# Pooled attention and four causal experts on one core: the same steps under two written-out orders

## The chip, the core and the metric

The kernel runs on one core of a Trainium2 chip. The core has a matmul engine (TensorE, PE in the profile; its weight loads are shown as PEld), VectorE (DVE), ScalarE (ACT), GpSimd (POOL) and SyncE (SP), each with an instruction stream of its own that runs in order and waits on semaphores; sixteen DMA engines move data. The metric is the device time of the program in microseconds. The kernel before took 159.37 us, the median of three runs (159.12 to 161.31).

## The reference

Inputs are q, k, v of 8 batches, 8 heads, 576 rows, 64 columns in fp32. First an attention whose keys and values are averaged over groups of eight rows, then a mixture of four small causal attention experts on its output x, of which each row uses the best two:

```python
def _attn_ref(q, k, v):
    k_p = k.reshape(B, H, Sp, pool, D).mean(axis=3)      # pool = 8, 72 keys
    v_p = v.reshape(B, H, Sp, pool, D).mean(axis=3)
    attn = softmax(scale * np.matmul(q, k_p.transpose(0, 1, 3, 2)))
    return np.matmul(attn, v_p)                          # becomes x: B, 576, 512
def _moe_ref(x, w_gate, wq, wk, wv, wo):
    logits = x @ w_gate                                  # 4 experts, the best 2 weigh in
    for e in range(E):
        q, k, v = x @ wq[e], x @ wk[e], x @ wv[e]        # 64 columns each
        a = softmax(causal(scale * (q @ k.transpose(0, 2, 1))))
        out += weight_of_e * (a @ v @ wo[e])
    return out                                           # B, 576, 512 in fp32
```

## The kernel before, in words

Each batch goes through a chain of some 140 small steps. A step is a Python function that issues a few instructions on one engine, and has a short name; `E1:2@46` is step E, part 1, of batch 2, with its PSUM banks 4 to 7. A letter d behind a copy puts it on DVE and not on ACT, a letter c behind a matmul step cuts it into tiles 32 columns wide.

- L_k, L_q, L_v (`load`, L118) are the loads of a batch, issued on POOL; they turn fp32 into bf16 on the way and write three rotating buffers a kind. W0 to W4 load the weights.
- PK, PV average k and v by a matmul; kc, kt, vc bring the result to SBUF. u (`turn`, L255) transposes q on DVE.
- E0, E1, E2 (`Es`) are the scores of rows 0 to 511 of one half of the heads, of the other, and of the last 64 rows of all (in batch 0: of rows 0 to 255, 256 to 511 and the rest); e00 to e21 (`es`, L292) their exponentials on ACT; D, d, x the sums and their inverses; O, o (`ov`, L338) the output x, transposed.
- P, p are the experts' q and k by pairs of experts; V, v their values and the gate's logits; g0 to g9 the gate; S, s (`sb`, L462) the experts' scores and exponentials; a (`am`, L479) the causal mask on POOL; B (`Bv`) the weighted values, bz, bg, b (L514 to L521) their scaling into the tile osc.
- osc must be transposed for the output projection. For batches 0, 1, 6 and 7 that is T (`flip`, L198, on PE) and a copy t; for batches 2 to 5 it is F (`crossbar`, L546 and L549), a transposing DMA issued on SP. F00 and F10 carry the main rows of the two expert pairs, F01 and F11 the last 64 rows.
- Y (`Y`) is the output projection of 128 rows (rows 512 to 575 of two batches share Y4), y (`y`, L180) the copy of its result into ofin, and with it the store on SP (`z`, L584, L580), 256 KB each. The last stores partly go out on ACT's queue.
- H is a warm-up: a matmul on a constant tile, whose result nothing reads (`warm_up`, L177).

All matmuls but the warm-ups and T stand on one helper line, L189. They come in tile shapes: 128*128 (rows by columns of the array) for P, V, B, T, Y and H, 64*128 for S, 32*128 for E, 96*32 for PK, PV, D and O.

The order in which steps are issued is one list of tokens, SEQ, written out in full, and a loop that calls each token's function. PE, ACT, DVE and POOL run their instructions in exactly that order (`manual_schedule`); SP's list follows the order of the F and y tokens. The list comes from a planner outside the kernel, which gives each step a cost and each buffer a time at which it is free; the kernel holds only its result. Batches overlap: while the experts of batch b run, the first attention of b+1 and b+2 is under way.

Of the kernel before, what the change touches and what calls it, by code (L numbers as in the profile page):

```python
# [21 lines left out]
def kernel(  # L22
# [553 lines left out]
    def z(b, c, queue):  # L576
# [17 lines left out]
        H1:0@0 u10:0 L_k2:1 u11:0 u01:0 E2:0@02 u00:0 E1:0@46 L_q0:1 e21:0 e20:0 e11:0 E0:0@02 L_q1:1 e10:0 PV:0@6  # L594
        L_q2:1 e01:0 vc:0d e00:0 c1:0d O11:0@6 L_q3:1 D1:0@7 c0:0d d1:0 O00:0@0 O20:0@1 O10:0@2 x1:0 D0:0@7 c2:0d W2:0
        O01:0@3 c3:0d D2:0@4 d0:0 H1:0@5 o11:0 d2:0 o10:0 W3:0 x2:0 x0:0 o20:0 P_q01:0@2 o00:0 L_v0:1 P_k01:0@1 p_q01:0
        o01:0 P_t0:0@0 p_k01:0 P_q11:0@2 L_v1:1 p_t0:0 P_q10:0@1 p_q11:0 L_v2:1 P_k11:0@0 p_q10:0 PK:1@2 p_k11:0 W4:0
        S02:0@4 kc:1 S03:0@0 S12:0@6 s02:0 P_k10:0@3 L_k0:2 kt:1d P_q00:0@2 u0:1 s03:0 L_k1:2 s12:0 H1:0@4 H1:0@4 u1:1
        a02:0 p_q00:0 p_k10:0d E2:1@04 L_k2:2 c4:0d E0:1@26 e20:1 e21:1 L_q0:2 V3:0@0 e01:1 V0:0@1 L_q1:2 v3:0d e00:1
        E1:1@46 a12:0 v0:0d V2:0@0 L_q2:2 e10:1 V1:0@1 v2:0d L_q3:2 PV:1@2 e11:1 v1:0d D0:1@0 a03:0 D2:1@3 vc:1d  # L600
        P_k00:0@4 L_v0:2 d0:1 D1:1@1 g1:0 O01:1@2 p_k00:0d x0:1 O00:1@0 L_v1:2 g2:0 S00:0@4 d1:1 o01:1 S10:0@6 x1:1
        O20:1@1 L_v2:2 g3:0 o00:1 O10:1@2 d2:1 s10:0 o10:1 O11:1@3 PK:2@0 L_k0:3 o11:1 x2:1 s00:0 S11:0@6 o20:1 L_k1:3
        S01:0@2 kc:2 P_t0:1@1 s11:0 g4:0 L_k2:3 kt:2d V2:1@0 p_t0:1d s01:0 V4:1@4 L_q0:3 v2:1d V3:1@1 u1:2 P_q0:1@0
        v4:1 L_q1:3 v3:1 g0:0 u0:2 a11:0 E1:2@24 p_q0:1 L_q2:3 g5:0 B11:0@1 g6:0 e10:2 g7:0 a10:0 P_k0:1@0 bz11:0
        L_q3:3 g8:0 g9:0 e11:2 bg11:0 E0:2@26 b11:0 a00:0 p_k0:1d L_v0:3 B10:0@1 e00:2 P_k1:1@4 bz10:0 a01:0 bg10:0
# [36 lines left out]
        e21:7 D0:7@0 b10:4 O00:7@2 e20:7 O20:6@6 d0:7 D1:7@7 O11:7@4 F10:4 o20:6 D2:7@1 O10:7@5 x0:7 g1:6 O20:7@0
        P_k0:6@6 d2:7 o00:7 x2:7 d1:7 P_t0:6@1 o20:7 x1:7 o01:7 P_k1:6@2 p_t0:6 o10:7 p_k0:6 B00:4@3 p_k1:6 S10:5@0
        bz00:4 S12:5@6 bg00:4 Y4:1@5 o11:7 s10:5 V4:7@2 b00:4 F11:4 s12:5 V0:7@4 y4:1d a10:5 F01:4 Y2:1@3 F00:4 v4:7d
        v0:7 S01:5@0 a12:5 y2:1d g0:6 S11:6@6 S11:5@4 s01:5 V3:7@2 g2:6 g3:6 V2:7@3 s11:6 v3:7d a01:5 Y3:3@0 v2:7d
        Y4:3@2 s11:5 y3:3d a11:6 V1:7@3 y4:3d B01:5@1 v1:7 S03:5@4 a11:5 S00:6@6 bz01:5 S01:6@2 s03:5 bg01:5 P_k0:7@0
        b01:5 s00:6 a03:5 g1:7 g2:7 B10:5@1 g4:6 p_k0:7 g5:6 a00:6 g6:6 Y3:2@6 s01:6 bz10:5 P_k1:7@7 bg10:5 b10:5 y3:2
# [83 lines left out]
```

## Time and profile before

| | |
|---|---|
| median of three runs | 159.37 us |
| the profiled execution | 159.26 us, span 157.6 us from the first to the last instruction |
| granted clock of the core, mean | 0.969 |
| PE, ACT, DVE, POOL busy | 91%, 85%, 79%, 57% of the span |
| read from HBM, written | 30.42 MB, 9.44 MB |

The profile is one execution. A busy PE there is not PE at its peak, since matmuls are pipelined and their ends are modelled; so starts of matmuls are compared, not lengths. A row of the chain of waits gives start, length and what the time went to; a row of the ordered list gives start, length, engine, line, operation, output and inputs, shape, and in brackets how long the engine stood idle before it and what ended that. The time of a run holds some 1.7 us around the span (159.26 - 157.6).

### The profile page before, as it was taken

The numbers are of one execution on the slowest core, as the hardware profiler recorded it, in microseconds if no ns is written. First come the engines' busy times: TensorE is split into PE (matmuls) and PEld (weight loads), VectorE is DVE, ScalarE is ACT, GpSimd is POOL, SyncE is SP. The second block draws the span as 40 slices with busy tenths as digits, with TensorE's granted clock in tenths as the row PEclk, the third lists the DMA queues.
The fourth block names the chain that finished last, engine by engine and source line by source line (L and its number), as shares of the span: only waits on it lengthen the run. The fifth ranks groups of instructions, "written<-read, shape, count | busy, mean of one in ns | idle before, by whom it ended". The sixth has DMA issues, their size and how long they took to land.

```text
span 157.6 us, 5500 instructions
## 1 busy us (share of the span) xinstructions
PE 143.9 (91%) x2155; PEld 82.8 (53%) x2155; DVE 124.4 (79%) x412; ACT 133.7 (85%) x249; POOL 90.5 (57%) x162
## 2 busy tenths in 40 slices
PE   6876798988999999999999899999999999999940
PEld 2333565545456356446545564857576665557620
DVE  1513567697999989998999889999998998898840
ACT  3016778999899999999999899999999999899740
POOL 6997479976989799897986342004500343533000
PEclk9998579999999999999999999999999999999996
DMA  2999999999999999999999994512213064487994
GB/s 19 161 173 180 181 179 179 188 179 182 180 182 180 180 180 181 178 249 181 180 245 249 179 148 108 37 50 60 80 28 104 8 177 131 124 320 264 344 354 146
DMA packets 70635, 26.20 MB, mean 166 GB/s; under 512 B 65744, under 2 KB 66000, under 8 KB 70608
## 3 DMA queue, kind: packets, MB, share of 16 engines
q0 software_dynamic: 60240, 15.21, 99.7%
q1 hardware_dynamic: 10144, 10.23, 21.2%
q10 hardware_dynamic: 224, 0.39, 0.9%
q8 instruction: 17, 0.28, 0.7%
q14 instruction: 10, 0.08, 0.2%
HBM read 30.42 MB, written 9.44 MB: 253 GB/s over the span
## 4 chain that ended last, share of the span: by engine, by line
PE 53%; DMA 23%; POOL 14%; issue 3%; DVE 2%; POOLq 0%; DVEq 0%
PE psum L189 52%; DMA kraw<-in_k_dram 18%; DMA qraw<-in_q_dram 5%; POOL kraw L118 4%; POOL vraw L118 3%; POOL qraw L118 3%; POOL etb L479 2%; PE psum L198 1%; POOL wst_q L131 1%; POOL wst_k L131 1%; DVE qT L255 1%; POOL wop L131 0%; DVE osc L521 0%; DVE ofin L180 0%; DVE G L406 0%
## 5 line engine op out<-in xcount | busy, mean ns | idle before, releaser
L462 ACT ACTIVATE etb<-psum 128x1024 bf16<-128x1024 f32 x48 | 47.6, 1033 | 1.1 <-PE psum L189 1.0
L479 POOL TENSOR_SCALAR_AFFINE_SELECT etb<-etb 128x256 bf16<-128x256 bf16 x64 | 25.5, 412 | 37.9 <-ACT etb L462 36.7
L292 ACT ACTIVATE eta<-psum 96x1024 bf16<-96x1024 f32 (+1 forms) x48 | 36.1, 812 | 4.7 <-PE psum L189 4.2
L118 POOL DMA_DIRECT2D qraw<-in_q_dram x32 | 21.2, 669 | 4.8 <-DMA vraw<-in_v_dram 2.2
L189 PEld LDWEIGHTS <-etb 128*128 128x128 bf16 x480 | 18.7, 97 | 7.2 <-issue 2.8
L338 DVE TENSOR_TENSOR xT<-psum,rza 128x512 bf16<-128x512 f32 x32 | 20.8, 684 | 1.7 <-ACT rza L315 1.4
L118 POOL DMA_DIRECT2D vraw<-in_v_dram x24 | 18.6, 777 | 6.2 <-DMA kraw<-in_k_dram 3.6
L189 PE MATMUL psum<-vaug,etb 128*128 128x65 bf16 x480 | 20.6, 193 | 0.1
L189 PE MATMUL psum<-xT,wqp 128*128 128x64 bf16 (+2 forms) x136 | 20.2, 282 | 0.1
L189 PE MATMUL psum<-wvg,xT 128*128 128x260 bf16 x144 | 20.0, 274 | 0.1
L189 PE MATMUL psum<-wop,oT 128*128 128x512 bf16 (+1 forms) x74 | 19.8, 374 | 0.2 <-DVE oT L180 0.2
L189 PE MATMUL psum<-xT,wkp 128*128 128x64 bf16 (+2 forms) x136 | 19.8, 279 | 0.0
L118 POOL DMA_DIRECT2D kraw<-in_k_dram x24 | 18.6, 785 | 1.7 <-POOLq L715 0.8
L521 DVE TENSOR_TENSOR osc<-psum,gt 128x256 bf16<-128x256 f32 (+2 forms) x40 | 16.5, 421 | 1.0
L189 PEld LDWEIGHTS <-xT 128*128 128x128 bf16 x144 | 12.7, 97 | 7.2 <-issue 3.7
L189 PE MATMUL psum<-qk 64*128 64x64 bf16 (+4 forms) x192 | 15.6, 277 | 0.2 <-ACT etb L462 0.2
L189 PE MATMUL psum<-eta,vp 96*32 96x64 bf16 (+2 forms) x272 | 14.1, 301 | 1.1 <-DVE vp L180 0.8
L189 PE MATMUL psum<-qT,kpT 32*128 32x64 bf16 (+2 forms) x272 | 12.7, 281 | 2.6 <-DVE qT L255 2.3
L255 DVE STREAM_TRANSPOSE qT<-qraw 128x576 f32<-128x576 f32 (+2 forms) x18 | 11.9, 690 | 3.7 <-DMA qraw<-in_q_dram 3.5
L180 ACT COPY ofin<-psum 128x512 f32<-128x512 f32 (+1 forms) x22 | 12.6, 591 | 1.6 <-PE psum L189 1.5
L180 DVE CAST qk<-psum 128x512 bf16<-128x512 f32 (+1 forms) x22 | 13.3, 611 | 0.7 <-PE psum L189 0.6
L315 ACT ACTIVATE rza<-rza 128x512 f32<-128x512 f32 (+1 forms) x24 | 12.5, 529 | 0.3
(75 smaller groups left out, 216.5 us busy)
## 6 DMA issues: line engine op xcount, KB each, us to landing
out_dram<-ofin SPq DMA_DIRECT2D x31, 256.0 KB, 3.5
kraw<-in_k_dram POOLq DMA_DIRECT2D x24, 192.0 KB, 7.8
qraw<-in_q_dram POOLq DMA_DIRECT2D x32, 144.0 KB, 7.6
vraw<-in_v_dram POOLq DMA_DIRECT2D x24, 192.0 KB, 7.2
out_dram<-ofin SPq DMA_DIRECT2D x7, 128.0 KB, 2.6
wst_q<-in_moe_wq_dram POOLq DMA_DIRECT2D x1, 256.0 KB, 7.4
wst_k<-in_moe_wk_dram POOLq DMA_DIRECT2D x1, 256.0 KB, 8.0
wst_v<-in_moe_wv_dram POOLq DMA_DIRECT2D x1, 256.0 KB, 8.3
```

Of the source, the lines that this page charges most:

```text
L118: nc.gpsimd.dma_start(out=dst, in_=src)
L131: nc.gpsimd.dma_start(out=dst, in_=src)
L180: (nc.vector.tensor_copy if dve else nc.scalar.copy)(out=out, in_=in_)
L189: nc.tensor.matmul(out=out, lhsT=lhsT, rhs=rhs, start=start, stop=stop)
L198: nc.tensor.transpose(out=out[s], in_=in_[:, s], identity=ident[0:n, 0:n])
L255: nc.vector.transpose(out=dst.rearrange("p (a s n) -> p a n s", s=32, n=2), in_=src.rearrange("p (a n d) -> p a n d", n=2, d=32))
L292: nc.scalar.activation(out=dst, in_=src, func=EXP, scale=ATT_EXP_SCALE)
L315: nc.scalar.activation(out=rz, in_=rz, func=EXP, scale=-1.0)
L338: nc.vector.tensor_tensor(out=xT[:, 2 * got[0][0] + t : 2 * got[-1][0] + t + 1 : 2, m + got[0][1].start : m + got[0][1].stop], in0=psum[:, ...
L462: nc.scalar.activation(out=et[:, ep, :, eo : eo + n], in_=psum[:, bank : bank + 2, 0:n], func=EXP, scale=MOE_EXP_SCALE,)
L479: nc.gpsimd.affine_select(out=blk, in_=blk, pattern=[[0, 2], [1, 128]], compare_op=ISGE, fill=0.0, base=0, channel_multiplier=-1,)
L521: nc.vector.tensor_tensor(out=osc(b, ep)[:, own, :].rearrange("p c (e d) -> p e c d", e=2), in0=o[:, :, :, 0:HD], in1=gt.to_broadcast([128 ...
```

## The change

Only SEQ changes: 1098 tokens become 1106. Every step of the old list is in the new one once, and eight warm-ups more (24 in place of 16), of which seven are in the form with 32 columns that the old list does not use. The first tokens, to the first loads of batch 1, are the same; behind them the order is different on every engine:

- In the planner, stores and crossbar transfers have a higher cost, a change of tile shape on PE has one, and output projections of older batches come earlier; the new list is what it then wrote. On PE the list changes shape 113 times before and 111 times after.
- Of the copies from PSUM, 29 move from DVE to ACT and 26 from ACT to DVE.
- Some PSUM banks are other ones.
- The order of the loads among themselves is the same; where they stand between POOL's masks is not.
- On SP, the six stores ahead of the first transfer were y1:0, y3:0, y0:0, y1:1, y3:1, y2:0 and are y3:0, y1:0, y2:0, y1:1, y0:0, y3:1; the transfers of batches 2 and 3 stand together, with only y0:2 between them.

The lines of both lists that hold the steps named below:

```diff
--- before
+++ after
@@ the list SEQ in the kernel @@
...
-        H1:0@0 u10:0 L_k2:1 u11:0 u01:0 E2:0@02 u00:0 E1:0@46 L_q0:1 e21:0 e20:0 e11:0 E0:0@02 L_q1:1 e10:0 PV:0@6
...
-        O01:0@3 c3:0d D2:0@4 d0:0 H1:0@5 o11:0 d2:0 o10:0 W3:0 x2:0 x0:0 o20:0 P_q01:0@2 o00:0 L_v0:1 P_k01:0@1 p_q01:0
...
-        E1:1@46 a12:0 v0:0d V2:0@0 L_q2:2 e10:1 V1:0@1 v2:0d L_q3:2 PV:1@2 e11:1 v1:0d D0:1@0 a03:0 D2:1@3 vc:1d
-        P_k00:0@4 L_v0:2 d0:1 D1:1@1 g1:0 O01:1@2 p_k00:0d x0:1 O00:1@0 L_v1:2 g2:0 S00:0@4 d1:1 o01:1 S10:0@6 x1:1
...
-        S01:0@2 kc:2 P_t0:1@1 s11:0 g4:0 L_k2:3 kt:2d V2:1@0 p_t0:1d s01:0 V4:1@4 L_q0:3 v2:1d V3:1@1 u1:2 P_q0:1@0
-        v4:1 L_q1:3 v3:1 g0:0 u0:2 a11:0 E1:2@24 p_q0:1 L_q2:3 g5:0 B11:0@1 g6:0 e10:2 g7:0 a10:0 P_k0:1@0 bz11:0
...
-        bg02:1 O10:3@0 b11:1 y3:0 PV:4@1 b02:1 s00:2 o10:3 a02:2 E0:4@26 vc:4d PK:5@0 L_k0:6 e01:4 g1:2 T11:1@4
...
-        L_q0:7 o00:4 y3:1 PV:5@6 y2:0 kc:6 L_q1:7 O01:4@7 S02:3@4 vc:5 o01:4 E0:5@02 a10:2 s02:3 L_q2:7 g7:2 V4:3@6
...
-        D0:5@5 bg11:2 O10:5@2 b11:2 e20:5 PK:7@3 vc:6d x1:5 F11:2 S10:3@0 d0:5 S12:3@6 F10:2 o10:5 V3:4@4 s10:3 kc:7
...
-        F11:3 y2:2 S01:4@0 a11:4 F10:3 p_t0:5d S00:4@4 S10:4@6 s01:4 g5:4 V4:5@2 g6:4 g7:4 g8:4 V3:6@3 s10:4 v4:5d
...
-        b11:4 V0:6@2 bz01:4 Y0:2@3 e10:7 bg01:4 b01:4 V2:6@0 y0:2d B10:4@1 v2:6 E2:7@46 v0:6 O01:7@3 bz10:4 bg10:4
...
-        g7:6 S10:6@4 F11:5 g8:6 a01:6 p_k1:7d g0:7 S02:6@0 S12:6@2 s10:6 B00:5@6 g9:6 g3:7 g4:7 g5:7 P_q0:7@7 s12:6
...
-        Y0:4@7 y0:3d s00:7 Y2:3@1 a10:7 B11:6@0 y0:4d S02:7@4 y2:3 a00:7 bz11:6 S11:7@2 bg11:6 S12:7@6 s02:7 b11:6
-        Y3:5@1 g8:7 g9:7 Y1:5@0 s11:7 y3:5d a02:7 Y4:5@4 B00:7@5 y1:5d B01:6@1 y4:5 a11:7 T11:6@2 s12:7 Y0:5@3 bz01:6
...
-        bz12:7 Y2:7@3 bg12:7 y3:7 b12:7 T02:6@6 T02:7@5 T12:6@2 T12:7@7 y2:7p t02:6d t02:7d t12:6d t12:7d Y4:7@0 z2:7
...
+        H1:0@0 H1:0@0 u00:0 H1:0@0 L_k2:1 u01:0 u10:0 E0:0@02 u11:0 L_q0:1 E1:0@46 e00:0 H1:0@0c L_q1:1 H1:0@0c H1:0@0c
...
+        O00:0@5 W2:0 O10:0@2 c2:0d e20:0 D0:0@3 o10:0 O20:0@0 d0:0 O11:0@1 D2:0@6 W3:0 o11:0 d2:0 x2:0 x0:0 P_q01:0@1
...
+        S03:0@0 S12:0@2 kc:1 s03:0 W4:0 P_k00:0@4 s12:0 kt:1d P_q10:0@5 L_k0:2 p_k00:0d P_q00:0@0 p_q10:0 P_k10:0@1
+        u1:1 L_k1:2 p_q00:0 P_k01:0@5 p_k10:0 u0:1 a12:0 E1:1@26 p_k01:0 E2:1@04 L_k2:2 e10:1 c4:0d H1:0@2c H1:0@2c
...
+        P_t0:1@1 g5:0 kt:2d L_q0:3 V3:1@2 v4:1d s02:0 P_q0:1@3 u1:2 L_q1:3 v3:1 u0:2 a11:0 E1:2@46 p_t0:1 p_q0:1 L_q2:3
...
+        O00:2@7 d2:2 kc:3 O10:2@2 x1:2 S02:1@0 o00:2 L_k2:4 S01:1@4 kt:3 B01:0@3 s02:1 o11:2 V2:1@7 L_q0:4 bz01:0 o10:2
...
+        p_q1:4 t02:0d u0:6 E2:5@06 D0:5@4 v1:4 PK:7@2 e21:5 g2:3 e20:5 D1:5@3 g3:3 d0:5 O10:5@5 kc:7 O00:5@0 d1:5
...
+        g4:4 V3:6@1 g1:5 g5:4 u1:7 Y0:2@0 s00:4 a01:4 B11:3@4 v3:6d V0:6@5 y0:2d s11:4 V2:6@1 a00:4 bz11:3 P_t0:5@6
+        bg11:3 g0:5 b11:3 v2:6 B01:3@0 a11:4 v0:6 p_t0:5d F10:3 S02:4@2 x2:6 bz01:3 S10:4@4 bg01:3 S03:4@6 s02:4
...
+        E1:7@26 bz11:4 bg11:4 Y4:1@0 b11:4 e10:7 a00:5 g2:6 Y0:1@4 y4:1d F11:4 Y2:3@1 e11:7 B10:4@5 y0:1d Y2:2@0 bz10:4
...
+        b10:5 y0:3 a00:6 B11:5@4 y2:4d g0:7 S03:7@0 S02:7@2 S12:6@6 s03:7 bz11:5 F11:5 Y3:2@5 bg11:5 b11:5 s12:6 a03:7
...
+        S10:7@0 bg10:6 s00:7 Y4:5@4 b10:6 g8:7 Y0:4@5 g9:7 s10:7 y4:5d Y3:3@6 a00:7 B11:6@7 y0:4d s01:7 Y3:4@4 a10:7
...
+        Y0:6@1 t02:6d t01:7 bz12:7 B02:7@4 bg12:7 y0:6 b12:7 Y3:7@5 bz02:7 t12:6 Y2:7@6 bg02:7 b02:7 y3:7 T02:7@4
+        T12:7@7 y2:7p t02:7d t12:7d Y4:7@0 z2:7 ya4:7 yb4:7d
```

More of the change, by code (lines that the diff above doesn't have):

```diff
@@ L643 @@
[L643 to L647, printed above, removed]
@@ new lines @@
+        p_q0:4d E0:5@02 g0:3 y0:0 u1:6 a11:3 T12:1@6 B10:2@4 L_v1:7 e00:5 P_k1:4@5 t12:1d bz10:2 bg10:2 e01:5 L_v2:7
+        b10:2 E1:5@06 p_k1:4d V3:4@4 a02:3 e10:5 kt:6d Y3:1@5 a01:3 v3:4d P_q1:4@2 e11:5 y3:1d T02:0@4 g1:3 V1:4@3
+        p_q1:4 t02:0d u0:6 E2:5@06 D0:5@4 v1:4 PK:7@2 e21:5 g2:3 e20:5 D1:5@3 g3:3 d0:5 O10:5@5 kc:7 O00:5@0 d1:5
+        S12:4@6 g4:3 B11:2@2 g5:3 x0:5 g6:3 g7:3 V2:4@3 x1:5 g8:3 bz11:2 g9:3 T02:1@4 o00:5 P_k0:4@1 s12:4 o10:5
+        B01:2@0 t02:1 v2:4 a12:4 bg11:2 p_k0:4 b11:2 S03:3@4 S00:3@6 bz01:2 D2:5@3 s03:3 F11:2 bg01:2 O01:5@2 b01:2
@@ new lines @@
+        PV:6@1 d2:5 s00:3 a03:3 o01:5 O20:5@3 O11:5@0 V0:4@4 F10:2 o11:5 vc:6 B10:3@2 a00:3 v0:4 kt:7d E1:6@06 x2:5
+        g0:4 F01:2 o20:5 V3:5@4 e11:6 bz10:3 bg10:3 P_k0:5@3 v3:5d e10:6 b10:3 E0:6@46 p_k0:5d F11:3 B00:2@2 e00:6 u0:7
+        V0:5@0 P_k1:5@3 bz00:2 e01:6 bg00:2 b00:2 B00:3@1 v0:5d p_k1:5 F00:2 E2:6@46 D0:6@0 bz00:3 bg00:3 e20:6 O10:6@3
+        b00:3 PV:7@2 e21:6 d0:6 g1:4 O01:6@4 F01:3 O00:6@1 vc:7d D1:6@5 x0:6 D2:6@0 O11:6@6 g2:4 V1:5@7 d1:6 o00:6
+        P_q0:5@2 x1:6 o01:6 d2:6 v1:5 V2:5@1 o10:6 p_q0:5 V4:5@0 o11:6 v2:5 S01:4@4 v4:5 S11:4@2 g3:4 S00:4@6 s01:4
@@ new lines @@
+        y2:3 B00:4@4 bg10:4 b10:4 y2:2 E2:7@26 D0:7@1 bz00:4 e20:7 D1:7@5 bg00:4 b00:4 O11:7@0 e21:7 F10:4 O20:6@2 d1:7
+        O01:7@3 O10:7@6 o20:6 O00:7@4 x1:7 g3:6 D2:7@5 O20:7@7 P_k0:6@2 g4:6 d0:7 o10:7 d2:7 P_k1:6@1 x2:7 o11:7 x0:7
+        o20:7 p_k0:6 B01:4@6 o01:7 p_k1:6 V4:7@7 o00:7 g0:6 S02:5@2 v4:7 S01:5@0 bz01:4 S10:5@4 bg01:4 s02:5 b01:4
+        V0:7@7 g5:6 F01:4 V3:7@6 g6:6 s01:5 v0:7d a02:5 P_q0:7@2 v3:7d s10:5 g7:6 F00:4 a01:5 V1:7@3 p_q0:7d P_t0:6@6
+        v1:7 g8:6 a10:5 S11:5@0 p_t0:6d S03:5@4 S12:5@2 s11:5 g9:6 P_k0:7@7 s03:5 V2:7@6 a11:5 s12:5 p_k0:7d Y1:3@0
@@ new lines @@
+        a03:5 v2:7d Y2:1@1 y1:3 S03:6@4 a12:5 S10:6@2 y2:1d S02:6@6 s03:6 Y4:3@0 s10:6 g1:7 a03:6 B01:5@1 y4:3d Y1:2@4
+        s02:6 a10:6 B00:5@5 bz01:5 bg01:5 b01:5 S01:6@2 y1:2 bz00:5 a02:6 S11:6@6 bg00:5 S00:6@0 s01:6 b00:5 P_k1:7@4
+        g2:7 F01:5 g3:7 s11:6 g4:7 P_t0:7@5 a01:6 p_k1:7d B10:5@2 s00:6 F00:5 p_t0:7d a11:6 Y0:3@3 bz10:5 Y2:4@5 bg10:5
+        b10:5 y0:3 a00:6 B11:5@4 y2:4d g0:7 S03:7@0 S02:7@2 S12:6@6 s03:7 bz11:5 F11:5 Y3:2@5 bg11:5 b11:5 s12:6 a03:7
+        P_q1:7@0 y3:2d s02:7 Y1:4@4 g5:7 a12:6 F10:5 g6:7 p_q1:7d B10:6@5 S00:7@6 y1:4 a02:7 S01:7@2 bz10:6 g7:7
@@ L660 @@
+        b02:6 y3:6 b11:7 Y0:7@5 bz01:7 Y1:7@4 bg01:7 b01:7 y0:7 T11:7@6 B12:7@3 y1:7d t11:7 T12:6@7 T02:6@2 T01:7@5
+        Y0:6@1 t02:6d t01:7 bz12:7 B02:7@4 bg12:7 y0:6 b12:7 Y3:7@5 bz02:7 t12:6 Y2:7@6 bg02:7 b02:7 y3:7 T02:7@4
+        T12:7@7 y2:7p t02:7d t12:7d Y4:7@0 z2:7 ya4:7 yb4:7d
     """
```

79 lines of the change are left out of this document (33 added, 46 removed).

## The prediction

> **What bounds the kernel now.** I read the page's busy shares, then its slices, then the busy time by stage, then what the matmul engine (PE) waited for, then the chain of work that ended last, and the ordered list of instructions at the places that these pointed to.
>
> ```profile
> span 157.6 us, 5500 instructions
> PE 143.9 (91%) x2155; PEld 82.8 (53%) x2155; DVE 124.4 (79%) x412; ACT 133.7 (85%) x249; POOL 90.5 (57%) x162
> PEclk9998579999999999999999999999999999999996
> DMA  2999999999999999999999994512213064487994
> ```
> ```profile
> 14.50:21.40 6.90, 5.79 (x84) 3.16 (x84) 3.75 (x9) 5.70 (x10) 3.88 (x6) 0.51 1.82 181
> 21.40:39.10 17.70, 16.33 (x253) 9.97 (x251) 12.90 (x36) 16.48 (x33) 14.44 (x23) 1.00 1.79 182
> 39.10:88.30 49.20, 48.76 (x800) 26.12 (x804) 46.03 (x148) 48.01 (x93) 42.20 (x71) 1.00 1.75 196
> 88.30:89.30 1.00, 0.28 (x21) 0.15 (x13) 1.00 (x3) 1.00 (x3) 0.77 (x1) 1.00 1.81 179
> 89.30:151.60 62.30, 62.08 (x914) 38.73 (x913) 55.59 (x195) 58.90 (x109) 16.36 (x41) 1.00 0.61 141
> ```
> The stage rows give length, then busy time of PE, its weight loads, DVE, ACT and POOL, then the granted clock, the DMA share and GB/s. From 39.1 us on PE is idle for 0.44, 0.72 and 0.22 us: it is the bound. The DMA engines are full to slice 24 (some 97 us) because the inputs stream in, and after that nearly empty until the stores. The digits 5 and 7 in the clock line are the 6.9 us at about half clock.
>
> ```profile
> PE psum L189 <- DVE qT L255: 0.7, 1, 0.7
> PE psum L189 <- DMA kraw<-in_k_dram: 0.7, 1, 0.7
> PE psum L189 <- DVE oT L180: 0.2, 1, 0.2
> ```
> ```profile
> 30.28 8.21 DMA qraw<-in_q_dram
> ...
> 78.11 11.13 DMA kraw<-in_k_dram
> ```
> ```profile
> 38.62 1.44 DVE L255 STREAM_TRANSPOSE qT<-qraw 128x576 f32<-128x576 f32 x2 [1.03 <-DMA qraw<-in_q_dram]
> ...
> 39.45 0.63 PE L189 MATMUL psum<-qT,kpT 32*128 32x512 bf16 x8 [0.74 <-DVE qT L255]
> ```
> Only three waits of PE are seen from 39.1 us on, and the first two are for loads. The chain says which: q of batch 2, issued at 30.28, lands at 38.49, and the step E1:2 starts behind it at 39.45; k of batch 7, issued at 78.11, lands at 89.24, and PK:7 waits for it. The third is at the end. So the run is: a start that ends at a load's landing (39.45), PE work without a hole to 88.3, a wait of 0.9, PE work without a hole to 151.6, and 6.0 us of last copies and stores.
>
> **The change, part by part.** No step is added or taken away but eight warm-up matmuls. I count each order's matmul columns with the time per column of these rows:
>
> ```profile
> 70.51 1.03 PE L189 MATMUL psum<-xT,wkp 128*128 128x512 bf16 x4
> 71.38 0.61 PE L189 MATMUL psum<-wvg,xT 128*128 128x260 bf16 x4
> 71.92 0.29 PE L189 MATMUL psum<-qT,kpT 32*128 32x64 bf16 x16
> ```
> Four matmuls of 512 columns take 71.38 - 70.51 = 0.87 us, 0.2175 each. Four of 260 (one V step) then take 0.44, and should let the next begin at 71.82; it begins at 71.92. That 0.10 us is the price of a change of tile shape (128*128 to 32*128).
>
> ```profile
> 25.49 1.43 DVE L255 STREAM_TRANSPOSE qT<-qraw 128x576 f32<-128x576 f32 x2
> ```
> ```profile
> kraw<-in_k_dram POOLq DMA_DIRECT2D x24, 192.0 KB, 7.8
> qraw<-in_q_dram POOLq DMA_DIRECT2D x32, 144.0 KB, 7.6
> ```
> *The start (to 39.45).* E0:0, E1:0, E2:0 come in another order, P_k00 and three more projections before E1:1 instead of behind it, eight warm-ups fill PE's holes. All this is ahead of E1:2, and E1:2 waits for q of batch 2, whose last chunk is the thirty-second load of a DMA queue that never runs dry; the order of the loads on POOL is unchanged. The E steps of batch 1 need the two turns of q that run from 25.49 on, so the first starts near 26.2. By columns the new order has 10.3 us of PE work from there to E1:2, 1.1 of it warm-ups, and 13 us for it. So I cost the whole start at 0: what covers it is the landing at 38.49. If the load came one chunk's time earlier (144 KB at the stage's 182 GB/s, 0.8 us), the gain is 0.8; if PE came late, the loss is told below.
>
> *PE work behind E1:2.* Every step behind it is the same but one: V2:1 is now behind, +0.44. Changes of tile shape behind it: 93 in the old order, 88 in the new one, -5 x 0.10 = -0.5. Together about 0. (Over the whole list 113 and 111; four of the 111 are those of the narrow warm-ups at the start.)
>
> *The wait for k of batch 7.*
>
> ```profile
> 76.53 4.23 SPq L584 DMA_DIRECT2D out_dram<-ofin  x4
> 88.44 1.18 SPq L546 DMA_TRANSPOSE oT<-osc  x1
> ```
> ```profile
> DMA to landing us min/median/max: 10.4/10.8/11.1
> ```
> Those three loads of k took 10.4 to 11.1 us where the median is 7.8: 3 us more, with the four stores of the row among them, so about 0.8 for a store. In the new order the early stores are y3:0, y1:0, then y2:0, y1:1, y0:0, y3:1. By columns (stretched by 48.9 / 46.8, measured over counted from 39.45 to 88.3) their projections stand at 63, 66, 78.8, 79.2, 82.8 and 86.4 us, and a copy and issue follow about 1 us later. So three, not four, compete with these loads, and the third not wholly: the landing moves from 89.24 to about 88.3. PE reaches PK:7 at 88.3 as before (59.9 us of columns are left there, 60.0 before). Bounds for the wait: 0 to 0.9 remain; I take 0.3, a gain of 0.6.
>
> *Copies moved between ACT and DVE.* 29 go to ACT, 26 to DVE; by kind ACT gets two vc, one p, one v more and a y less.
>
> ```profile
> L180 ACT COPY ofin<-psum 128x512 f32<-128x512 f32 (+1 forms) x22 | 12.6, 591 | 1.6 <-PE psum L189 1.5
> ```
> At about 0.59 each that is +1.8 us for ACT and as much less for DVE. ACT is idle for 1.2 + 3.4 us in the two long stages; it stays below PE. Cost 0 while that slack lasts; without it up to 1.8.
>
> *Output projections forward, crossbar transfers and stores on SP.*
>
> ```profile
> oT<-osc SPq DMA_TRANSPOSE x16, 2.4
> ```
> Y2:3, Y1:3, Y4:1, Y4:5 and Y0:3 come earlier, Y0:1, Y2:1, Y4:3 and Y3:3 later. SP works its list in order. New on it: the mains of batch 3 (F10:3, F00:3) stand behind the store of y0:2 and are wanted by Y2:3 some 9 us later: no wait. F11:5 stands behind the stores of y0:3 and y2:4; behind it F10:5 and all later stores. By columns its data are ready some 14.5 us before PE's end and Y4:5 starts 12.3 before it; the transfer lands 2.4 after its issue, so the margin is -0.2, about 0. A transfer holds SP for 1.18 us (row above), which all later stores then carry.
>
> *The end.*
>
> ```profile
> 145.50:149.50 4.00, 4.00 (x68) 2.82 (x67) 3.57 (x18) 3.09 (x7) 0.00 (x0) 1.00 0.97 330
> 149.50:153.50 4.00, 1.93 (x17) 0.92 (x13) 1.75 (x10) 1.95 (x4) 0.00 (x0) 1.00 0.99 367
> ```
> ```profile
> 150.60 0.48 DVE L180 COPY oT<-psum 128x64 bf16<-128x64 bf16 x4 [0.16 <-PE psum L198]
> 150.94 0.70 PE L189 MATMUL psum<-wop,oT 128*128 128x256 bf16 x4 [0.22 <-DVE oT L180]
> ...
> 151.68 0.42 DVE L180 COPY ofin<-psum 128x256 f32<-128x256 f32 x1 [0.59 <-PE psum L189]
> ...
> 153.18 0.64 SPq L580 DMA_DIRECT2D out_dram<-ofin  x1
> ```
> The last projection waits for four small copies; in the new order two of them are done earlier, so the wait is shorter by two of them: -0.2. The DMA engines are full at 367 GB/s, 0.71 us for a store of 256 KB, to 153.5: stores queue, and the last goes out at 153.18 though its copy ended at 152.10. In the last 10 us of PE work the old order has 15 projections, the new one 13; in the last 3.2 us both have six. So the queue is shorter when the end begins, but the last six make most of it anew. Bounds: nothing, or the whole lateness of the last store, 1.1; I take 0.4.
>
> **Sum.** The profiled run took 159.26 us for a span of 157.6, 0.11 below the median of the three runs. 159.26 + 0 (start) - 0.06 (PE work) - 0.6 (k of batch 7) - 0.2 (copies at the end) - 0.4 (stores) = 158.0; on the median's scale 158.1.
>
> **The rivals.**
> *No gain.* If the stores near 80 us cost the loads as much as before and the last six stores fill the queue anyway, only 0.06 + 0.2 go: 159.1. For it: PE has no other hole to close, and six stores in the last 3.2 us stand as they stood.
> *A free end.* If the store queue is empty when the last copy ends, the last store goes out at 152.2, 1.0 earlier, and lands as the small ones do, not as the large ones:
>
> ```profile
> out_dram<-ofin SPq DMA_DIRECT2D x31, 256.0 KB, 3.5
> ...
> out_dram<-ofin SPq DMA_DIRECT2D x7, 128.0 KB, 2.6
> ```
> That is -1.0 - 0.9 in place of -0.4: 156.6. Against it: 0.97 and 0.99 in the rows.
> *A new wait on the way.* F11:5 late for Y4:5, or ACT's 1.8 us more in a stretch where it is full (48.01 of 49.20): +0.5 to +2 over the forecast, 159.5 as the middle. For it: the margin of nothing on SP. Against it: 16.4 us of POOL in the last stage and 3.4 us of idle ACT.
> *Slower: the half clock lasts.* The E steps of batch 0 leave PE mostly idle; in the trace the clock falls to 0.51 from 14.5 to 21.4 us. The new order puts warm-ups there, four of them only 32 columns wide. If these count for little and the clock stays halved, PE loses half of that time: from P_q01:0 to E1:2 it has 15.1 us of columns. Its slack before E1:2 is some 2.5 us, so the end moves only when the halved stretch goes on for more than 5 us beyond 21.4; to 35 us it loses 6.8 - 2.5 = 4.3: 162.4. Against it: the old order, with fewer fillers, was back at full clock by 21.4.
> [...]
>
> **How the numbers follow.** Forecast, 157.5 to 158.8: 0.50. No gain, 158.8 to 159.4: 0.20. New wait, 159.4 to 161: 0.13. Free end, 156 to 157.3: 0.10. Half clock, 160 to 163: 0.07. The range 156.6 to 160.8 leaves out a third of the free end, most of the half clock and a tail of the new wait, and some for what I have not thought of. About 2% is what a measurement of this kernel can tell from no change: below 156.2 lies a small part of the free end, 0.06; above 162.5 a part of the last two, 0.07; within, 0.87.
>
> **What would show it.** E1:2 at 39.4 (start worth nothing); PE's wait for kraw near 88 us at 0.3 or less; PE without a hole from there to its last matmul near 150.8; the last store out within 0.7 of its copy. I am wrong if E1:2 starts more than 0.5 us earlier or later, if PE waits for oT or for ACT in the middle, or if the stretch behind the last matmul is not between 5.0 and 6.1 us.

## The result, and the profile after

The new order takes 160.57 us, the median of 20 runs, against 159.44 us for the old one (20 runs). The ratio is 1.0052, 95% interval 1.003 to 1.0075: slower by half a per cent, about 0.8 us, where the prediction had a gain of 1.3. The ratio leaves out the four executions of the new order that are over 1.5% above its fastest, the profiled one with 162.39 us among them, while the medians hold all 20. So a second trace of the new order (159.71 us, run e15 below) is read beside the first, and against it a second trace of the old order (159.02 us, run e12).

The page of the new order, its first trace:

```profile
span 160.6 us, 5513 instructions
PE 144.9 (90%) x2163; PEld 82.8 (52%) x2163; DVE 123.1 (77%) x408; ACT 135.5 (84%) x253; POOL 90.1 (56%) x162
PEclk9999999599999999999999999999999999999996
```
The page of its second trace:

```profile
span 158.0 us, 5513 instructions
PE 144.6 (91%) x2163; PEld 82.8 (52%) x2163; DVE 123.0 (78%) x408; ACT 135.5 (86%) x253; POOL 90.5 (57%) x162
PEclk9999999999999999999999999999999999999995
```
ACT has 1.8 us more work, as counted, and DVE 1.4 less. The half clock of the old order's first trace, 14.5 to 21.4 us, is gone in both; the first trace of the new order has a shorter one later, from 27.93 to 31.34 us.

Stages of the second trace, cut as for the old order (length, then PE, its weight loads, DVE, ACT and POOL busy, clock, DMA share, GB/s):

```profile
39.10:88.30 49.20, 49.12 (x765) 26.84 (x764) 45.96 (x145) 48.80 (x87) 44.13 (x76) 1.00 1.77 191
88.30:89.30 1.00, 1.00 (x40) 0.61 (x42) 0.99 (x4) 1.00 (x5) 0.00 (x0) 1.00 1.40 290
89.30:138.50 49.20, 49.16 (x759) 29.97 (x746) 43.21 (x147) 47.73 (x99) 12.25 (x31) 1.00 0.45 102
138.50:139.50 1.00, 0.51 (x4) 0.18 (x3) 0.75 (x4) 1.00 (x2) 0.54 (x3) 1.00 0.61 124
```
PE no longer stands still at 88.3; it does at 138.5, half of that microsecond. ACT, 48.01 of 49.20 before, is at 48.80: it has hardly any slack left.

What PE waited for from 36 us to its end (the view lists idle stretches of more than 0.15 us), in the second trace of the new order:

```profile
PE psum L189 <- DMA oT<-osc: 0.5, 1, 0.5
PE psum L189 <- DVE xT L329: 0.3, 1, 0.3
PE psum L189 <- DVE oT L180: 0.2, 1, 0.2
```
and in the second trace of the old order:

```profile
PE psum L189 <- DVE qT L255: 0.9, 1, 0.9
PE psum L189 <- DMA kraw<-in_k_dram: 0.8, 1, 0.8
PE psum L189 <- DVE oT L180: 0.2, 1, 0.2
```
The wait for k (kraw) is gone and a wait for a transposed tile (oT) has come. This is where it came in the first trace of the new order, seen first in SP's queue and then on PE:

```profile
135.22 1.12 SPq L546 DMA_TRANSPOSE oT<-osc  x1
136.43 1.22 SPq L549 DMA_TRANSPOSE oT<-osc  x1
137.74 1.01 SPq L584 DMA_DIRECT2D out_dram<-ofin  x2
138.80 1.13 SPq L546 DMA_TRANSPOSE oT<-osc  x1
```
```profile
140.33 0.39 PE L189 MATMUL psum<-wop,oT 128*128 128x512 bf16 x1
141.88 0.39 PE L189 MATMUL psum<-wop,oT 128*128 128x512 bf16 x1 [1.16 <-DMA oT<-osc]
```
The chain of waits of that trace has the step between them:

```profile
138.80 3.04 DMA oT<-osc
```
F11:5 is issued at 138.80, behind two other transfers and the stores of y0:3 and y2:4, and lands 3.04 later. Y4:5's first matmul, which does not need it, starts at 140.33, its second at 141.88.

**The two second traces set against each other** (e15 less e12, starts of matmuls; 158.0 - 157.3 = +0.7). E1:2 starts at 39.52 and 38.88: +0.64. From there to the last matmul 112.68 and 112.12: +0.56. From the last matmul to the end 5.81 and 6.32: -0.51. The middle term, by start-to-start times of PE against their columns: Y4:5 +0.67; PK:7 -0.94; V2:1 +0.44; 88 changes of tile shape for 93, 8.64 us for 9.24, -0.60; waits between 0.03 and 0.24 us, 13 of them with 1.44 us for 7 with 0.60, +0.83; +0.16 not assigned. (Waits given with two digits below are of this kind, between starts; the views above count from the modelled end of a matmul and show the same wait of Y4:5 as 0.5.)

### The profile page after: what moved, and what is told of

It is laid out like the page before. It is cut to its first block, busy times and chain, and to the rows that moved or that the text cites. A ratio compares the mean times of both kernels' runs of the same rounds, so it can differ in the third digit from the quotient of the medians.

```text
span 160.6 us, 5513 instructions
## 1 busy us (share of the span) xinstructions
PE 144.9 (90%) x2163; PEld 82.8 (52%) x2163; DVE 123.1 (77%) x408; ACT 135.5 (84%) x253; POOL 90.1 (56%) x162
## 4 chain that ended last, share of the span: by engine, by line
PE 72%; DMA 12%; POOL 5%; ACT 3%; DVE 2%; issue 1%; SPq 1%; ACTq 0%; POOLq 0%; DVEq 0%
PE psum L189 69%; DMA qraw<-in_q_dram 6%; DMA wst_q<-in_moe_wq_dram 5%; DMA oT<-osc 2%; PE psum L198 2%; POOL qraw L118 2%; POOL kraw L118 2%; POOL vraw L118 1%; ACT etb L462 1%; PE psum L177 1%; ACT ofin L180 1%; DVE xT L338 1%; ACT eta L292 1%; SPq L584 1%; DVE qT L255 0%
## 5 line engine op out<-in xcount | busy, mean ns | idle before, releaser
L462 ACT ACTIVATE etb<-psum 128x1024 bf16<-128x1024 f32 x48 | 47.1, 1029 | 1.2 <-PE psum L189 0.9
L189 PE MATMUL psum<-vaug,etb 128*128 128x65 bf16 x480 | 21.1, 194 | 0.0
L189 PE MATMUL psum<-wvg,xT 128*128 128x260 bf16 x144 | 20.7, 278 | 0.0
L189 PE MATMUL psum<-xT,wqp 128*128 128x64 bf16 (+2 forms) x136 | 19.1, 279 | 0.8 <-DVE xT L338 0.8
L189 PE MATMUL psum<-qT,kpT 32*128 32x64 bf16 (+2 forms) x272 | 13.2, 288 | 1.9 <-DVE qT L255 1.8
L180 DVE CAST qk<-psum 128x512 bf16<-128x512 f32 (+1 forms) x21 | 12.7, 611 | 2.3 <-PE psum L189 1.9
L189 PE MATMUL psum<-eta,vp 96*32 96x64 bf16 (+2 forms) x272 | 13.0, 281 | 1.5 <-DVE vp L180 1.1
L177 PE MATMUL psum<-warm 128*128 128x512 bf16 (+1 forms) x41 | 11.8, 437 | 2.3 <-DVE onesd L147 1.3
L180 ACT COPY ofin<-psum 128x512 f32<-128x512 f32 (+1 forms) x21 | 11.9, 581 | 1.6 <-PE psum L189 1.0
```

Of the source, the lines that this page charges most:

```text
L177: nc.tensor.matmul(out=psum[rows, bank, :], lhsT=warm[:, rows], rhs=warm[:], start=True, stop=True)
L180: (nc.vector.tensor_copy if dve else nc.scalar.copy)(out=out, in_=in_)
L189: nc.tensor.matmul(out=out, lhsT=lhsT, rhs=rhs, start=start, stop=stop)
L462: nc.scalar.activation(out=et[:, ep, :, eo : eo + n], in_=psum[:, bank : bank + 2, 0:n], func=EXP, scale=MOE_EXP_SCALE,)
```

## The experiments

Each kernel is an edit of SEQ; B is the new list, A the old one. Ratios are to runs of the old order on the same chip, with 95% intervals; experiments in different groups of runs stood on different chips, so their ratios are compared, not their times.

**The transfer and the projection that waits for it (e1, e5).**

```diff
e1:
- b10:5 y0:3 a00:6 B11:5@4 y2:4d ... bz11:5 F11:5
+ b10:5 F11:5 y0:3 a00:6 B11:5@4 y2:4d ... bz11:5
```


> The new order with one token moved: the transfer F11:5 stands on SP ahead of the stores of y0:3 and y2:4, directly behind b10:5, which writes its data. Theory (the order loses in two places: the projection Y4:5 waits 1.3 us for that transfer, and the start reaches E1:2 about 1.5 us late): PE's wait for oT near 140 us goes from 1.3 us to 0.2 or less and the time falls by 1.0 to 1.3 us against the new order, to about 159.4, ratio to the old one 0.997 to 1.000. Rival (the store queue at the end sets the time, and whatever PE loses before it is only waited for elsewhere): the wait goes but the last stores land as late as before, time at most 0.4 us shorter, ratio 1.003 to 1.005.

Measured: 160.08 us, ratio 1.0032 (0.9994 to 1.0069). In SP's list the transfer came out ahead of only one of the two stores (y0:3's copy, on ACT, is still put before it), was issued at 136.84 and landed 2.92 later. Y4:5 waits 0.77 us. Neither theory is decided: the transfer still stood behind one store.

```diff
e5: e1's edit, and
- Y4:5@4 ... y4:5d ... Y3:4@4 ... y3:4
+ Y3:4@4 ... y3:4d ... Y4:5@4 ... y4:5
```


> The new order with the transfer F11:5 one store earlier on SP (as in e1_f115_first) and the projections Y4:5 and Y3:4 changed about on PE, so that Y4:5 is issued some 2 us later and Y3:4, whose transfers landed long before, in its place. Theory (Y4:5 waits for the landing of F11:5, and PE then has no other hole before the end): the wait near 139 to 140 us, 1.33 us in the new order and 0.77 in e1_f115_first, is gone, and the whole gain is kept to the end: 1.2 to 1.4 us under the new order, 0.6 to 0.8 under e1_f115_first, so near 159.3, ratio to the old order 0.995 to 1.000. Rival (the stores at the end set the time): the wait is gone, the last store goes out earlier but lands no earlier than in e1_f115_first, ratio 1.002 to 1.004.

Measured: 159.67 us, ratio 0.9995 (0.996 to 1.0029). PE's listed waits from 39.3 us on are down to these:

```profile
PE psum L189 <- DVE oT L180: 0.2, 1, 0.2
PE psum L189 <- issue: 0.2, 1, 0.2
```
The loss of 0.5% is gone with that one wait: the ratio goes from 1.0052 to 0.9995, some 0.9 us, and the two intervals do not meet. Two other pairs that differ by the same edit went the same way, e7 to e6 on one chip (1.0061 to 1.0007) and e2 to e9 (1.0053 to 1.0023), each with intervals that overlap. (The edit also exchanges the engines of the copies y4:5 and y3:4.) The store queue did not take the gain back: the rival of e1 falls. But the new order with its wait mended is no faster than the old one. Nor is there much room: the next transfer, F10:5, is late for its projection by 0.86 us in e6's trace.

**The list cut at E1:2 (e2, e3, e9).**

```diff
e2: A up to E1:2, B behind it
e3: B up to E1:2, A behind it (V2:1 with it)
e9: e2 with e5's edit
```


> The old list up to E1:2, the new list behind it (V2:1 is ahead of E1:2, as in the old order). Theory: E1:2 at 39.4, no wait for kraw near 88 us, still the wait of 1.3 us for oT near 140; against the old order +1.3 - 0.9 - 0.5 (tile shapes) + some 0.3 of small waits, so a ratio of 0.998 to 1.003, and the spread of runs as narrow as the old order's. Rival (the rest is what costs, through more work on ACT or the stores, and the start is worth nothing): ratio 1.004 to 1.008, as the new order.

> The new list up to E1:2, the old list behind it, with V2:1 and the copies p_t0:1 and v2:1 put in behind E1:2. Theory: E1:2 near 40.5 to 41, the wait for kraw shrinks by as much as PE comes later, no wait for oT near 140; 1.0 to 1.5 later at E1:2, +0.44 for V2:1, -0.9 of the kraw wait: +0.5 to +1.2 us, ratio 1.003 to 1.008, with the wide spread of the new order's runs. Rival (the start is worth nothing because E1:2 waits for the load of q): ratio 0.999 to 1.001.

Measured: e2 160.32 us, ratio 1.0053 (1.002 to 1.0086); e3 160.07 us, 1.0018 (0.9979 to 1.0057). The rest alone brings the whole loss, as e2's rival had it for the place, though not for the reason; the start alone brings too little to be told from none. In e2's trace Y4:5 waits 1.26 us, the clock was halved for 10.24 us from 15.42 on, and E1:2 came at 41.17, 2.77 behind the landing of its load: the old start can lose too. In e3's trace E1:2 came at 39.08.

> The old list up to E1:2 (as in e2_old_start_new_rest), behind it the new list with F11:5 one store earlier on SP and Y4:5 changed about with Y3:4 (as in e5_y45_later). Theory (the new order loses at Y4:5 and by its start, each in its own place, and gains at the wait for kraw): e2 less 0.9 to 1.3 us, so 159.0 to 159.4, ratio to the old order 0.995 to 0.999, faster than the old order by what the kraw wait was worth less the small new waits. Rival (the old start is hit by the half clock as often as the new one, and the gain behind E1:2 is given back): ratio 1.000 to 1.003, as e5_y45_later.

Measured, e9: 159.68 us, ratio 1.0023 (0.999 to 1.0056). Not the gain that was expected: its trace has the k wait gone, Y4:5's gone, five fewer shape changes, and needs from E1:2 to the last matmul 111.97 us, the old order's first trace 111.93. The small waits (13 with 1.40 us; there 6 with 0.50) and a wait of 0.40 for xT at 48 us stand against it in the trace.

**The clock in the start (e4, e8, e7, e6, e10).**

```diff
e4:  - H1:0@2c H1:0@2c H1:0@2c             (ahead of E0:1)
e8:  - the same three, and the four H1:0@0c of batch 0
e7:  + H1:0@3 x6 ahead of E1:1; H1:0@5 x4 for e4's three
e6:  e7 and e5      e10: e6 with five ahead of E1:1, and ten more at PV:0, O01:0, P_q01:0
```


> The new order without the three narrow warm-ups that stand on PE between E2:1 and E0:1 (nothing reads their result). Theory (they are part of what makes the start late: the three stand behind ACT's e10:1, whose bank they write, and take 1.4 us at half clock, 0.7 at full clock, ahead of E0:1): E1:2 comes 0.7 to 1.4 us earlier and the time falls by as much, ratio 0.996 to 1.001. Rival (they keep the clock up, as they were put in to do): the half clock lasts longer, E1:2 is not earlier, ratio 1.005 or above.

> The new order without its seven narrow warm-ups (four in the E steps of batch 0, three ahead of E0:1); nothing reads their result. Rival of the prediction (warm-ups 32 columns wide count for nothing, and the clock is what decides): clock and time as in the new order, 160.4 to 160.8. Theory (they count, and the full clock from 14.5 to 21.4 us is of their making): the clock is halved early in the start as in the old order; if PE still meets E1:1 when its load lands, the time is equal or, since the later window then comes less often, up to 0.7 us shorter; if PE comes late to E1:1 it is up to 2 us longer. I take 160.6, with no more than the same time as likeliest.

> The new order with the start of e6_wide_fill_and_y45 alone; its tail, with the wait of Y4:5, is as it was. Theory: median as that of the new order's runs with a full clock in the start, 159.8 to 160.1, ratio 1.002 to 1.004, and a narrow spread. Rival (the half clock is hidden): 160.4 to 160.8 as the new order, ratio 1.004 to 1.008.

> As e5_y45_later, and in the start six wide warm-ups (128 columns) on bank 3 directly ahead of E1:1, where PE waits for the turned q of batch 1, and four wide ones on bank 5, which nobody holds, in place of the three narrow ones ahead of E0:1. Theory (the wide spread of the new order's runs is a window of half clock that falls between 24 and 31 us in about half of them, because PE is idle for some 2.5 us there, and that PE time is on the path): no run has its clock halved in the start, mean clock 0.99 or above in nearly all of them, and the median falls to that of the undisturbed-clock runs, 158.5 to 158.9, ratio 0.993 to 0.997. Rival (the half clock comes from something else, or is hidden as in the old order): same share of runs with a clock under 0.988, median as e5_y45_later.

> As e6_wide_fill_and_y45 (five warm-ups ahead of E1:1 instead of six), and besides three narrow warm-ups on bank 1 ahead of PV:0, three wide ones on bank 7 ahead of O01:0 and four ahead of P_q01:0, where PE is idle for 0.7, 0.8 and 1.0 us. Theory (a half-clock window comes behind a stretch with too much idle PE time; in e6's traced run it came at 21.9 us, behind such holes): hardly a run with a clock under 0.985, E1:2 near 39.1 in all of them, median 158.6 to 159.2, ratio 0.993 to 0.998. Rival (it is not the clock but the landings of q and the weights, which come earlier or later by a microsecond from run to run): clock high in all runs and the median still 159.5 to 160.0 with the same spread.

Measured: e4 160.45 us, 1.0028 (0.9987 to 1.0069); e8 161.23 us, 1.0106 (1.0069 to 1.0142); e7 160.41 us, 1.0061 (1.0027 to 1.0096); e6 159.99 us, 1.0007 (0.9976 to 1.0038); e10 159.87 us, 1.0036 (0.9999 to 1.0072). The clock of e8, and below it of e10:

```profile
PEclk9999557999999999999999999999999999999997
```
```profile
PEclk9999999999999999999999999999999999999985
```
Without the narrow warm-ups the clock is halved for 10.24 us in e8's trace and none of its eight runs has a mean clock above 0.976, where nineteen of the new order's twenty have 0.98 or more: the warm-ups 32 columns wide did count here. The kernel is slower without them than was expected (160.6), though its interval just overlaps that of the new order. With fillers in every hole (e10) eleven of twelve runs have a mean clock of 0.987 or more, and yet the median is not under e5's and the runs still spread from 159.04 to 161.03. So the theory that a stretch of half clock makes the new order's spread and loss falls; at most it is a part, and where the spread comes from stays open. The gains expected of e4 and e7 are not there or not to be told from none.

**The stores beside the loads of k (e11), and the old order again (e12).**

```diff
e11: A with Y2:0 y2:0 Y3:1 y3:1 moved from ahead of PK:7 to behind Y0:1
     (in other banks, and y3:1 as y3:1d)
```


> The old order with two of its four stores near 76 to 81 us moved behind PK:7: Y2:0 and Y3:1 with their copies and stores now stand behind Y0:1, PE's 0.87 us for them with them. Step 3 of the prediction (each of the stores holds up the loads of k of batch 7 by about 0.8 us): the landing moves from 89.2 to about 87.6, PE comes to PK:7 at 87.0 to 87.5 and waits 0.1 to 0.5 us, time 0.4 to 0.8 us under the old order, ratio 0.995 to 0.998. Rival (the stores cost the loads nothing, the three late loads have another reason): landing near 89.2, a wait of 1.5 to 1.8 us, ratio 1.000 to 1.003.

Measured, e11: 159.74 us, ratio 1.0009 (0.9976 to 1.0042). The three loads of k of batch 7, from issue to landing, in the old order again (e12), in e11 and in the new order's second trace:

```profile
DMA to landing us min/median/max: 10.7/11.0/11.3
```
```profile
DMA to landing us min/median/max: 8.7/8.8/9.0
```
```profile
DMA to landing us min/median/max: 6.3/6.6/9.5
```
Two stores fewer are worth 2.2 us, 1.1 each: the step holds. The new order's first two loads, at 6.3 and 6.6, go with it: its stores of this time are issued only from 80.65 on, and the third load takes 9.5. In e11 the landing came at 87.55 and PK:7 did not wait for it. But the time did not fall: without Y2:0 and Y3:1 in their old place PE comes to PV:5 sooner, and waits there 0.7 us (at 79 us) until ACT has emptied its bank; it waits for ACT once more, 0.3 us, at 94 us.

```profile
PE psum L189 <- ACT etb L462: 1.1, 2, 0.7
```


> The old order once more, for a second trace of it. If E1:2 is bound by the landing of q of batch 2, it starts within 0.5 us of 39.4 whatever the clock did between 14 and 26 us; if by PE, it comes later by half of what the clock lost beyond 6.8 us. The wait for kraw near 88 us should be there again, 0.3 to 1.0 us.

Measured, e12: 159.02 us, one run, full clock from the start, E1:2 at 38.88, 0.97 behind the landing of q at 37.91 (0.96 in the first trace, 39.45 behind 38.49). In the old order the start is bound by that load, and the 6.8 us of half clock from 14.5 on cost nothing.

**The copies moved (e13, e14), and the new order again (e15).**

```diff
e13: e5 with 54 copies on A's engines (y4:5 is there already), as
     - y0:3 y2:4d y3:2d   + y0:3d y2:4d y3:2
e14: A with all 55 on B's engines
```


> As e5_y45_later, but each of the 55 copies that changed engine is again on the engine that the old order has it on; the order is as in e5_y45_later. Open: the traces of the new order show a dozen waits of PE of 0.03 to 0.24 us behind E1:2, 1.3 us together, where the old order has six with 0.5. Theory (they come from the copies moved, step 4 of the prediction, which was costed at nothing): they fall to 0.5 to 0.8 us in all and the time by about 0.6, to 159.0, ratio 0.994 to 0.998. Rival (they come from the order in which PE takes the steps, each now closer behind the step that it needs, and the new copies fit the new order): 1.3 us or more stay, ratio 1.000 to 1.004.

> The old order with the 55 copies on the engines that the new order has them on; nothing else is changed. Theory (copies moved cost): small waits of PE grow from 0.5 to 1.0 us or more and the time by 0.3 to 0.8, ratio 1.002 to 1.005. Rival (the engine of a copy matters only where the order makes it tight): small waits within 0.3 us of 0.5, ratio 0.999 to 1.002.

Measured: e13 168.35 us, ratio 1.055 (1.0495 to 1.0606); e14 168.46 us, 1.056 (1.05 to 1.0621). Both theories miss by far. What PE waits for in e13 (first lines):

```profile
PE psum L189 <- DVE osc L521: 1.1, 3, 0.6
PE psum L189 <- DVE xT L338: 0.7, 2, 0.4
PE psum L189 <- ACT L L180: 0.7, 2, 0.4
```
The engine of a copy and its place in the order belong together: some 55 of them set to the other list's choice, with not a step more, cost 9 us in either list. So the small waits cannot be put down to the copies' engines alone by such an edit; that question stays open.

> The new order once more, for a second trace on a chip on which other runs stand. If the wait of Y4:5 and the small waits are its own, they are there again: 1.0 to 1.7 us for the transfer near 139 us, 1.2 to 1.5 us of small waits; E1:2 between 39.0 and 41 with the clock of the start; time 159.8 to 160.8, ratio 1.003 to 1.008.

Measured, e15: 160.18 us, ratio 1.0064 (1.0023 to 1.0106); Y4:5 waits 0.67 us, small waits 1.44 us, E1:2 at 39.52. The wait is the order's own; its size varies from trace to trace (0.67, 1.03, 1.12, 1.26, 1.33, 1.71 in e15, e4, e8, e2, the first trace and e7).

## Why the prediction was wrong

The forecast added gains of 1.26 us and put three terms at nothing: the start, the margin of F11:5, and the small waits of PE. In the two second traces the gains came to 1.6 us, and the three terms took 2.1.

*The start, costed at 0: failed.* "E1:2 waits for q of batch 2" no longer holds. In the new order's second trace the load lands at 38.01, as early as before, and E1:2 comes 1.51 behind it, not 0.97. DVE goes from a copy into the turn of q, 0.56 behind the landing, and PE is itself busy with another step up to 39.44 (38.42 + 1.02); the old order's second trace below it has PE idle until the turn is done:

```profile
38.42 1.02 PE L189 MATMUL psum<-xT,wqp 128*128 128x512 bf16 x4
38.51 0.15 DVE L180 COPY L<-psum 128x4 f32<-128x4 f32 x1
38.57 1.43 DVE L255 STREAM_TRANSPOSE qT<-qraw 128x576 f32<-128x576 f32 x2
39.40 0.24 PEld L189 LDWEIGHTS <-kpT 32*128 32x128 bf16 x8 [0.44 <-DVE qT L255]
39.52 0.63 PE L189 MATMUL psum<-qT,kpT 32*128 32x512 bf16 x8
```
```profile
38.88 0.63 PE L189 MATMUL psum<-qT,kpT 32*128 32x512 bf16 x8 [0.93 <-DVE qT L255]
```
The failed sentence is "10.3 us of PE work from there to E1:2 ... and 13 us for it". Whatever the count is worth, PE does not run these columns without holes. Waits of the second trace from 26 to 41 us:

```profile
PE psum L189 <- DVE qT L255: 1.3, 1, 1.3
PE psum L177 <- ACT eta L292: 0.8, 1, 0.8
PE psum L189 <- DVE vp L180: 0.5, 1, 0.5
PE psum L189 <- DVE xT L329: 0.3, 1, 0.3
```
The first line ends at 26.50, when the E steps of batch 1 start. The other three, 1.5 us, lie behind it, and PE changes its tile shape twelve times from there to E1:2, some 1.2 us at 0.10 each, which a count of columns does not hold. With the 10.3 of the count these are the 13.0 us from 26.50 to 39.52: the slack, 2.5 or more by the forecast, is used up. The chain runs PE, ACT, DVE and back, and columns see only one of the three. The second line is the narrow warm-ups themselves, which stand behind ACT's e10:1. Without a halved clock E1:2 comes 1.2 to 1.8 behind the landing in five traces of the new start (e1, e3, e15, and e7 and e10 with more warm-ups) and 0.97 in the old start (e12). It is 0.96 in e4, without the narrow warm-ups, but there the load landed later, at 38.56, and E1:2 started at 39.52 as in e15. Where a stretch of half clock falls near 28 us it is 2.8 in the new order's first trace, and 2.1 in e9 and 1.3 in e11, both with the old start. Yet e3 shows no loss from the start that its interval could tell from none; +0.64 is a reading of two traces, not a measured effect.

*F11:5, "margin -0.2, about 0", put into a rival: failed in size.* The mechanism was named, with a chance of 0.13 and a price of 0.5 to 2; it is what happened, and the 160.57 us lie in that rival's band. The margin let the transfer go out when its data are ready and land 2.4 later. In the first trace its last data were written at 136.83, by this row (b10:5):

```profile
136.27 0.56 DVE L521 TENSOR_TENSOR osc<-psum,gt 128x384 bf16<-128x384 f32 x1
```
It went out at 138.80, behind 2.0 us of SP's other work, and took 3.04. In the second trace these are 135.03, 136.46 (1.4 us of SP's work) and 2.92. Y4:5 could have used it 3.7 us behind its data in both, not 2.2 as the columns had it; so without the queue even a flight of 3.0 would have been in time, and with the queue and the median flight of 2.4 it would have been 0.1 and 0.7 us late. The queue, which the prediction named and did not price, makes the transfer late, and the longer flight makes up the rest. The rival's own argument, "the margin of nothing", should have made it the forecast: by e5 it carries the whole measured loss.

*PE without a hole: failed.* The sum had no term for small waits. They grew from 0.60 to 1.44 us, 0.06 to 0.2 each, most of them until ACT or DVE had done something by the trace's semaphore events, in a list that has ACT at 48.80 of 49.20 us. With the start, this is where the two traces say that the gains went, and why e5 and e9, with both large waits gone, would only draw level. It is a sum over traces: no edit takes the small waits away by themselves.

*Right.* The wait for k: -0.6 forecast, -0.94 between the two second traces. The mechanism is the one stated (e11; 1.1 us for a store, not 0.8), and the last load landed at 88.17 for 88.3 forecast. But PE also came to PK:7 only at 89.09, for 87.42 in the old order. At its old time it would still have waited, by an estimate 0.2 us (88.17 less the 88.88 - 0.94 at which the old order wanted the load). That nothing of the wait remained is thus in part luck: PE was late. Five fewer shape changes: -0.5 forecast, -0.60. V2:1: +0.44, as counted. Copies: +1.8 us on ACT, as counted. The end: 5.81 us behind the last matmul, inside 5.0 to 6.1. *Half right.* The last stores go out without delay behind their copies:

```profile
152.67 0.37 ACT L180 COPY ofin<-psum 128x256 f32<-128x256 f32 x1 [0.54 <-PE psum L189]
153.06 0.47 SPq L580 DMA_DIRECT2D out_dram<-ofin  x1
153.07 0.54 ACTq L580 DMA_DIRECT2D out_dram<-ofin  x1
```
and the stretch is 0.51 shorter where 0.4 was forecast; but the two small copies done earlier gave nothing: the last projection waits 0.40 us (0.38 before).

By the forecast's terms: -1.26, then start +0.64, Y4:5 +0.67, small waits +0.83, not assigned +0.16, the copies at the end +0.2, k -0.34, shapes -0.1, stores -0.11: +0.7, which is the difference of the two second traces.

*The clock.* Half clock lasted 6.83 us in the old order's first trace, 3.41 in the new order's and 10.24 in those of e2 and e8. Either order shows it ahead of E1:2 in one trace and not in the other: the new one from 27.93 on in its first trace and not in e15, the old one from 14.5 on in its first and not in e12. In the 3.41 us ahead of it PE was idle for 1.8 us in the new order's first trace and for 1.5 in the old order's; the latter hold the E steps of batch 0, which leave PE idle for less than half of the time, not "mostly". The rival "the half clock lasts" is not what happened: with the added warm-ups the clock was full from 14.5 to 21.4 in both traces of the new order, though not in e5's, which has the same start and half clock from 20.21 on. Nor was more than 5 us of half clock beyond 21.4, as the rival had it, needed for an E1:2 that comes late: with the one stretch of 3.41 us at 28 us it is 1.4 us later than in the other trace.

## What to carry to other kernels

A step that is one in-order queue away from late is late: add the queue ahead of it (here 1.4 and 2.0 us of SP's work), and the longest flight seen of its kind (here 2.92 and 3.04 us), not the median of all (2.4). A resource's work by count is a lower bound (here 10.3 us of PE for 13.0 in the trace); where three engines are nearly full and hand each other small pieces, take from a trace what the holes between them sum to, and expect a new order to have its own. Before believing in a removed wait, ask what next small wait it uncovers: here the small waits grew by 0.8 us, in a dozen pieces.

## What the runs showed of the hardware

- Half clock came behind a stretch without any long hole of PE. In the first trace of the new order the clock falls at 27.93; in the 3.41 us ahead of it PE was idle for 1.8 us, in two holes. The first ends at 26.55; the second starts at 27.51, so that 0.42 us of it lie ahead of the fall, and ends at 28.28 (idle time in brackets):

```profile
26.55 0.96 PE L189 MATMUL psum<-qT,kpT 32*128 32x512 bf16 x24 [1.38 <-DVE qT L255]
...
28.28 1.44 PE L177 MATMUL psum<-warm 128*32 128x512 bf16 x3 [0.77 <-ACT eta L292]
```
The second trace has holes of 1.33 and 0.77 us at the same two places, and full clock. So these traces give no length of hole that halves the clock.

- With the seven narrow warm-ups (32 columns) the clock was higher: without them it is halved for 10.24 us in e8's trace, and the mean clock of its eight runs is 0.957 to 0.976, for 0.98 or more in nineteen of twenty with them.
- A store of 256 KB issued beside three loads of 192 KB put off their landings by 1.1 us each: 11.0 us with four stores (e12), 8.8 with two (e11), 6.7 in the new order's first trace, where the next store is issued at 82.00, 2.7 us behind the last of the loads.
- A transposing transfer of 64 columns, F11:5, issued right behind two stores took 2.68 to 3.08 us to land in six traces (the first, e15, e2, e4, e7, e8), where the median of all 16 is 2.4. Behind one store it took from 2.25 (e5) to 3.18 (e9), so that the stores are its cause is not shown.
